# Attention and gated MLP in one kernel: background matmuls dealt one pair to an exp, and layer norm by row tile on GpSimd

## The chip, the cores and the metric

The kernel runs on one core of a Trainium2 chip. The metric is the time of one execution on the device in microseconds (us). Engines are named as in the profile: PE is TensorE's matmuls, PEld its weight loads, DVE is VectorE, ACT ScalarE, POOL GpSimd, and SP the queue that issues the DMAs here.

## The reference

```python
x  = A_x                                  # [1, 2048, 512], bf16
xn = (x - mean) / sqrt(var + 1e-5)        # over the 512 columns
q, k, v = split(xn @ wqkv)                # 32 heads of 16 columns
o  = softmax(q @ k.T / 4) @ v             # per head, 2048 keys
A  = merge_heads(o) @ wo
B  = (relu(xn @ W_gate) * (xn @ W_up)) @ W_down    # 1792 columns inside
out = x + A + B
```

## The kernel before, in words

The sequence of 2048 rows is held as 4 blocks of 512 rows (c4 for queries, b for keys) and 16 row or key tiles of 128 (m, kt). The 32 heads form 4 groups (gg) of two halves (ee) of four heads (j). A head has 16 columns, and two heads share 32 partitions of kT, so kT keeps two copies of k, each with the other head's 16 rows set to zero by a mask (hmask).

The main loop runs over 2048 score tiles (c4, gg, ee, kt, j), each 128 keys by 512 queries. Three tiles make a **unit**; there are 683. For a unit TensorE computes three scores into one half of ps_sc (three banks of PSUM, two halves), ScalarE takes the exp of all three in one instruction into a slot of `ring` (11 slots), and later TensorE multiplies the ring slot with v (PV) into bank 0 of ps_b, where four heads stand at four column places of the array. v has a column of ones, so PV gives the softmax sums too. After 16 key tiles `normalise` copies bank 0 to o_sb, sends the sums through DRAM to all partitions (DMAs rsum, rec_scr and rb), and GpSimd multiplies (oT).

All else is **background** and goes through bank 1 of ps_b: the projections of q and k, the GLU (for each c4, 14 tiles ft of four matmuls with W_up, then four with W_gate), and the output rows (for each 128 rows, 14 matmuls with W_down and 8 with wo). `mm_chain` issues such a chain in operations of two matmuls; I call such an operation a pair. A tile in bank 1 is emptied by VectorE before the next chain starts. In the last block the output rows are summed in parts: a first part without the last head group into `resid`, then the last matmul at the end.

The first units also hold the layer norm of the four blocks (`ln_block`), the transposes of xn, k of the first group and all of v.

What sets the order is a planner. Each operation is recorded with its engine, an estimated duration, its dependencies and a priority; `Graph.run` places them one by one on each engine by these estimates, and the engines then run exactly that order, each waiting on semaphores. Scores have priority u - 2000 and PV u + 4 (PV_LAG), so PV may be late by as much as the ring allows. A background chain gets one priority in units (`later(p, lead, fn)`), and one of its dependencies is the exp of unit p - lead.

## Time and profile before

| | |
|---|---|
| three runs | 1050.02, 1044.48, 1049.61 us; median 1049.61 |
| profiled execution | 1046.26 us, of which the span of the trace is 1044.5 us |
| busy share of the span | ACT 89%, PE 83%, DVE 18%, POOL 5% |
| mean granted TensorE clock | 0.805 |
| exps (ACT, `ring<-ps_sc`, L711) | 683, 929.2 us busy; ScalarE idle before them 69.6 us |
| score matmuls (L699), PV (L729) | 2048 each, 318.0 and 304.3 us busy |
| GLU matmuls (L500, wus and wgs) | 224 each |

The span runs from the first to the last instruction of the trace. Busy time of an engine is the union of its instructions. In a row of the timeline stand the start and duration in us, the engine, the line, the operation, the tile written and those read, and in brackets how long the engine was idle before it and what released it. In a row by stages stand the stretch, its width, and for each engine the busy time with the count of instructions, then the granted TensorE clock (1.00 is full speed), the DMA share and GB/s.

### The profile page before, as it was taken

Reading aid. Unit: us, or ns where it says so; the run is one execution under the profiler, and the core shown is the slowest. Engines: PE = TensorE matmul, PEld = TensorE weight load, DVE = VectorE, ACT = ScalarE, POOL = GpSimd, SP = SyncE. Lnnn points to the kernel's source line nnn. Section 1 sums busy time; section 2 is a strip of 40 time slices with the busy share of each in tenths; the row PEclk is TensorE's granted clock in tenths of the full one; section 3 lists DMA queues with packets and bytes.
Section 4 is the critical chain, followed back from the end, with each engine's and each line's share of the span. In section 5 each row is a group of like instructions: output and inputs, shape, how many; then the busy total and the mean of one; then the engine's idle time right before and its main releaser. Section 6 shows DMA issues by size and latency. Waiting matters only on the chain.

```text
span 1044.5 us, 11864 instructions
## 1 busy us (share of the span) xinstructions
PE 863.8 (83%) x5152; PEld 205.5 (20%) x5152; DVE 191.1 (18%) x323; ACT 932.4 (89%) x687; POOL 51.1 (5%) x46
## 2 busy tenths in 40 slices
PE   4888888888898887888889888888889988888894
PEld 1221221211132111111122111111112212121121
DVE  8732231311002111111001111111100212120001
ACT  3699999999889999999988999999998899999980
POOL 3000000000000000000000000000000000000000
PEclk9998896976599777878569887787758989895587
DMA  8011101110011111100011101111001211110000
GB/s 231 2 31 28 28 18 31 41 31 11 22 36 37 31 36 36 26 21 17 11 31 45 43 12 31 36 31 31 11 21 31 52 42 46 32 26 10 8 26 31
DMA packets 84067, 34.58 MB, mean 33 GB/s; under 512 B 69936, under 2 KB 79920, under 8 KB 84016
## 3 DMA queue, kind: packets, MB, share of 16 engines
q1 hardware_dynamic: 84016, 33.83, 12.4%
q8 instruction: 40, 0.66, 0.3%
q14 instruction: 11, 0.09, 0.0%
HBM read 31.20 MB, written 2.36 MB: 32 GB/s over the span
## 4 chain that ended last, share of the span: by engine, by line
ACT 58%; PE 33%; DMA 4%; DVE 3%; issue 1%; POOL 0%; POOLq 0%; SPq 0%
ACT ring L711 58%; PE ps_b L500 18%; PE ps_sc L699 9%; PE ps_b L729 6%; DMA rb<-rec_scr 2%; DMA rsum<-o_sb 1%; DMA rec_scr<-rrec 1%; DMA wus<-in_B_W_up_dram 1%; DVE stats L442 1%; DVE pid L371 1%; DVE v_aug L533 0%; POOL oT L681 0%; PE ps_sc L500 0%; DVE o_sb L663 0%; DVE kT L525 0%
## 5 line engine op out<-in xcount | busy, mean ns | idle before, releaser
L711 ACT ACTIVATE ring<-ps_sc 128x1536 bf16<-128x1536 f32 (+1 forms) x683 | 929.2, 1555 | 69.6 <-PE ps_sc L699 55.0
L699 PE MATMUL ps_sc<-qT,kT 32*128 32x512 bf16 x2048 | 318.0, 460 | 133.3 <-ACT ring L711 126.4
L729 PE MATMUL ps_b<-ring,v_aug 128*17 128x512 bf16 x2048 | 304.3, 455 | 1.2 <-DVE o_sb L663 1.2
L699 PEld LDWEIGHTS ps_sc<-qT,kT 32*128 32x128 bf16 x2048 | 68.0, 93 | 442.4 <-ACT ring L711 342.6
L729 PEld LDWEIGHTS ps_b<-ring,v_aug 128*17 128x17 bf16 x2048 | 61.8, 89 | 199.4 <-issue 187.6
L595 DVE COPY up_sb<-ps_b 128x512 f32<-128x512 f32 x56 | 38.7, 691 | 315.7 <-PE ps_b L500 315.7
L500 PE MATMUL ps_b<-xnT,wus 128*128 128x512 bf16 x224 | 90.8, 505 | 1.8 <-DMA wus<-in_B_W_up_dram 1.7
L681 POOL TENSOR_TENSOR oT<-o_sb,rb 128x512 bf16<-128x512 f32 x32 | 40.5, 1266 | 956.4 <-DMA rb<-rec_scr 927.1
L500 PE MATMUL ps_b<-xnT,wgs 128*128 128x512 bf16 x224 | 73.8, 421 | 1.9 <-DMA wgs<-in_B_W_gate_dram 0.5
L500 PE MATMUL ps_b<-Wd,hT 128*128 128x512 bf16 x224 | 63.8, 414 | 8.0 <-POOL oT L681 6.3
L599 DVE SCALAR_TENSOR_TENSOR hT<-ps_b,up_sb 128x512 bf16<-128x512 f32 x56 | 38.7, 691 | 105.9 <-PE ps_b L500 105.9
L663 DVE COPY o_sb<-ps_b 128x512 f32<-128x512 f32 x32 | 22.1, 692 | 160.6 <-PE ps_b L729 160.3
L500 PE MATMUL ps_b<-Wo_p,oT 128*128 128x512 bf16 x125 | 33.4, 383 | 0.0
L631 DVE TENSOR_TENSOR ost<-ps_b,xr_sb 128x512 bf16<-128x512 f32 x12 | 8.3, 691 | 116.4 <-PE ps_b L500 116.4
L525 DVE TENSOR_SCALAR kT<-ps_b,hmask 128x512 bf16<-128x512 f32 x32 | 22.5, 746 | 22.1 <-PE ps_b L500 22.1
L500 PEld LDWEIGHTS ps_b<-Wd,hT 128*128 128x128 bf16 x224 | 18.4, 101 | 40.5 <-issue 16.0
L500 PEld LDWEIGHTS ps_b<-xnT,wus 128*128 128x128 bf16 x224 | 14.5, 103 | 39.8 <-issue 33.7
L500 PEld LDWEIGHTS ps_b<-xnT,wgs 128*128 128x128 bf16 x224 | 13.8, 99 | 35.3 <-DVE up_sb L595 19.4
L500 PE MATMUL ps_b<-xnT,Wk 128*128 128x512 bf16 x64 | 18.9, 405 | 1.8 <-DVE xnT L480 0.8
L500 PE MATMUL ps_b<-xnT,Wq 128*128 128x512 bf16 x60 | 19.2, 416 | 0.8
L500 PE MATMUL ps_b<-Wv,xnT 128*128 128x512 bf16 x64 | 16.4, 381 | 1.9 <-DVE v_aug L533 1.0
L512 DVE CAST qT<-ps_b 128x512 bf16<-128x512 f32 x15 | 10.3, 689 | 30.6 <-PE ps_b L500 30.6
(43 smaller groups left out, 108.3 us busy)
## 6 DMA issues: line engine op xcount, KB each, us to landing
rb<-rec_scr SPq DMA_DIRECT2D x32, 256.0 KB
wus<-in_B_W_up_dram SPq DMA_DIRECT2D x56, 128.0 KB, 3.0
wgs<-in_B_W_gate_dram SPq DMA_DIRECT2D x56, 128.0 KB, 2.3
xr_sb<-in_A_x_dram SPq DMA_DIRECT2D x16, 128.0 KB, 2.2
out_dram<-ost SPq DMA_DIRECT2D x16, 128.0 KB, 1.7
Wd<-in_B_W_down_dram SPq DMA_DIRECT2D x1, 1792.0 KB, 11.7
x_sb<-in_A_x_dram SPq DMA_DIRECT2D x3, 512.0 KB, 5.9
x_sb<-in_A_x_dram SPq DMA_DIRECT2D x2, 256.0 KB, 3.0
```

The costliest lines, as they stand in the source:

```text
L371: G.op("DVE", 100, lambda e: e.tensor_scalar(pid[:], pid[:], 16, None, op0=ALU.bitwise_and), reads=[t_pid], writes=[t_pid], prio=-890)
L442: G.op("DVE", 620, lambda e, m=m: e.bn_stats(stats[:, m, :], xs(m)), reads=[t_xm[m]], writes=[t_st], prio=pr)
L500: ins = e.matmul(bank_of(tile, sub), l(), r(), start=(i == 0), stop=(i == n - 1))
L512: G.op("DVE", 690, lambda e: e.tensor_copy(qT[:, tq.slot, :], bank_of(t, sub)), reads=[t], writes=[tq], prio=prio)
L525: G.op("DVE", 690, lambda e, ee=ee, dst=dst: e.tensor_scalar(dst, bank_of(t, sub), hmask[:, ee:ee + 1], None, op0=ALU.mult), reads=[t, t_m ...
L595: G.op("DVE", 690, lambda e: e.tensor_copy(up_sb[:, tup.slot, :], bank_of(tu)), reads=[tu], writes=[tup], prio=pr)
L599: G.op("DVE", 690, lambda e: e.scalar_tensor_tensor(out=hT[:, FT * th.slot + ft, :], in0=bank_of(tg), scalar=0.0, in1=up_sb[:, tup.slot, : ...
L663: G.op("DVE", 690, lambda e: e.tensor_copy(o_sb[:, to.slot, :], ps_b[:, 0, :]), reads=[tp], writes=[to], prio=-950, name="oev%d" % n)
L681: G.op("POOL", 1200, lambda e: e.tensor_tensor(oT[:, tn.slot, :], o_sb[:, to.slot, :], rb[:, trb.slot, :], ALU.mult), reads=[to, trb], wri ...
L699: ins = e.matmul(ps_sc[:, 3 * ts.slot + i, :], kT[32 * j:32 * j + 32, 2 * gg + ee, 128 * kt:128 * kt + 128], qT[32 * j:32 * j + 32, t_q[(c ...
L711: return e.activation(ring[:, UNIT * tr.slot:UNIT * tr.slot + n, :], ps_sc[:, 3 * ts.slot:3 * ts.slot + n, :], ACTF.Exp, scale=0.25)
L729: ins = e.matmul(ps_b[32 * j:32 * j + VN, 0, :], v_aug[:, kt, 8 * gg + 2 * j + ee, 0:VN], ring[:, UNIT * tr.slot + i, :], start=(kt == 0), ...
```

## The change

**One pair to a unit.** `job(want, n, fn, lead)` takes the place of `later`. All background chains are sorted by the unit at which they are wanted, and each pair gets a slot of its own, one unit behind the one before at the least. The slot is the pair's priority, and `after` makes the pair depend on the exp of the unit before the slot. The output rows of a block take 11 slots for each 128 rows, from unit 10 of the next block on. Those of the last block come before its end: a part with five of the eight head groups, a part with two, and at the end the last one. The GLU's places are moved too.

**PV by key tile.** The four PV matmuls of a key tile (j = 0 to 3) are issued together once the fourth is exponentiated, in place of three for each unit. The ring has 13 slots.

**Layer norm by row tile.** The addition of eps, the power and the normalisation are done by GpSimd for each row tile apart; in block 0 ScalarE copies each tile's transposes out of PSUM. Before, VectorE normalised and the power was done once for four tiles.

**k split by GpSimd.** VectorE copies k to `kp` once, and GpSimd writes the two masked copies. Before, VectorE wrote both from PSUM.

**Start.** TensorE runs 14 matmuls of zeros at first. The memsets of v_aug's ones and of Wo_p wait for the exps of units 1 and 29, and so does the load of Wd for the latter. The first load of x is split in two. Eight of the oT tiles use the space of x_sb, and the output tiles that of xn_sb.

```diff
-NRING = 11
+NRING = 13
...
+            if o.after is not None and int(o.after) > 0:
+                o.order.add(self.units[min(int(o.after), len(self.units)) - 1])
...
-        G.op("POOL", 2500, lambda e: e.memset(v_aug[:, :, :, DH:VN], 1.0), writes=[t_vones], prio=-500)
-        G.op("POOL", 4200, lambda e: e.memset(Wo_p[:], 0.0), writes=[t_woz], prio=-400)
+        G.op("POOL", 2500, lambda e: e.memset(v_aug[:, :, :, DH:VN], 1.0), writes=[t_vones], prio=-500, after=2)
+        G.op("POOL", 4200, lambda e: e.memset(Wo_p[:], 0.0), writes=[t_woz], prio=20, after=30)
...
-            G.op("DVE", 150, lambda e: e.tensor_scalar(vare[:, sl], mv[:, sl, 1], EPS, None, op0=ALU.add), ...
-            G.op("POOL", 1000, lambda e: e.tensor_tensor(rstd[:, sl], vare[:, sl], expo[:, :], ALU.pow), ...
+                G.op("POOL", 100, lambda e, m=m: e.tensor_scalar(vare[:, m:m + 1], mv[:, m, 1:2], EPS, None, op0=ALU.add), ...
+                G.op("POOL", 300, lambda e, m=m: e.tensor_tensor(rstd[:, m:m + 1], vare[:, m:m + 1], expo[:, 0:1], ALU.pow), ...
...
-                    G.op("DVE", 420, lambda e, m=m, t=t_n: e.tensor_scalar(
+                G.op("POOL", 450, lambda e, m=m, t=t_n: e.tensor_scalar(
                         xn_sb[:, t.slot, :], xs(m), mv[:, m, 0:1], rstd[:, m:m + 1], op0=ALU.subtract, op1=ALU.mult),
...
+            G.op("DVE", 690, lambda e: e.tensor_copy(kp[:, tkp.slot, :], bank_of(t, sub)), reads=[t], writes=[tkp], prio=prio)
+                G.op("POOL", 450, lambda e, ee=ee: e.tensor_scalar(dsts[ee], kp[:, tkp.slot, :], hmask[:, ee:ee + 1], None, op0=ALU.mult), ...
...
+            for _ in range(14):
+                ins = e.matmul(ps_b[:, 1, :], zeros[:, 0:128], zeros[:], start=True, stop=True)
...
-            a = upos(c4) + (40 if c4 == 0 else 28)
-            z = upos(c4 + 1) - (12 if c4 < NB - 1 else 50)
+            a = upos(c4) + (20 if c4 == 0 else 60)
+            z = upos(c4 + 1) - (8 if c4 < NB - 1 else 56)
             for ft in range(FT):
-                later(a + (z - a) * ft / FT, 8, lambda pr, od, c4=c4, ft=ft: glu(c4, ft, pr, od))
+                job(a + (z - a) * ft / FT, 4, lambda s, c4=c4, ft=ft: glu(c4, ft, s))
             for i in range(4):
                 if c4 < NB - 1:
-                    later(upos(c4 + 1) + 8 + 4 * i, 6, lambda ...: out_rows(c4, i, pr, od, range(8), True, True))
+                    job(upos(c4 + 1) + 10 + 12 * i, 11, lambda ...: out_rows(c4, i, range(8), True, True, slots=s), 2)
                 else:
-                    later(upos(c4, 3, 1, 0) + 8 + 4 * i, 6, lambda ...: out_rows(c4, i, pr, od, range(7), True, False))
+                    job(upos(c4 + 1) - 54 + 10 * i, 10, lambda ...: out_rows(c4, i, range(5), True, False, slots=s), 2)
+                    job(upos(c4 + 1) - 12 + i, 1, lambda ...: out_rows(c4, i, [5, 6], False, False, slots=s), 1)
+        jobs.sort(key=lambda j: j[0])
+        plan, cur = [], 0.0
+        for want, n, fn, lead in jobs:
+            s = []
+            for _ in range(n):
+                cur = max(cur, want)
+                s.append(cur)
+                cur += 1.0
+            plan.append((s[0] - lead, s, fn))
...
-                G.op("PE", 330 * (i1 - i0) / 3, pv, reads=[tr, t_vones] + [...], writes=[tp], prio=u + PV_LAG, name="pv%d" % u)
+            for i, t in enumerate(cl):
+                where[t] = (tr, i)
+                if t[4] == 3:
+                    pv_group(t[:3], t[3], u)
```

In the three excerpts of the order below, a row is a line of the kernel, an operation, the tile written and those read, its size, and how many stand in a row. Before, L699 is the scores, L729 PV and L500 the background; now they are L760, L736 and L510.

TensorE's order at the output rows of c4 = 1, which stand some ten units into c4 = 2, before:

```order
L729 MATMUL ps_b<-ring,v_aug 17x512 x3
L500 MATMUL ps_b<-Wd,hT 128x512 x2
L699 MATMUL ps_sc<-qT,kT 128x512 x3
L500 MATMUL ps_b<-Wd,hT 128x512 x4
L699 MATMUL ps_sc<-qT,kT 128x512 x3
L500 MATMUL ps_b<-Wd,hT 128x512 x4
L699 MATMUL ps_sc<-qT,kT 128x512 x3
L500 MATMUL ps_b<-Wd,hT 128x512 x4
L500 MATMUL ps_b<-Wo_p,oT 128x512 x2
L699 MATMUL ps_sc<-qT,kT 128x512 x3
```

and now:

```order
L736 MATMUL ps_b<-ring,v_aug 17x512 x4
L760 MATMUL ps_sc<-qT,kT 128x512 x6
L510 MATMUL ps_b<-Wd,hT 128x512 x2
L736 MATMUL ps_b<-ring,v_aug 17x512 x4
L760 MATMUL ps_sc<-qT,kT 128x512 x3
L510 MATMUL ps_b<-Wd,hT 128x512 x2
L736 MATMUL ps_b<-ring,v_aug 17x512 x4
L760 MATMUL ps_sc<-qT,kT 128x512 x3
```

Between two groups of scores stood up to six background matmuls and no PV; now there are two, and PV goes on between them.

TensorE's order at the end of the program, before:

```order
L699 MATMUL ps_sc<-qT,kT 128x512 x2
L500 MATMUL ps_b<-Wd,hT 128x512 x10
L500 MATMUL ps_b<-Wo_p,oT 128x512 x7
L729 MATMUL ps_b<-ring,v_aug 17x512 x12
L500 MATMUL ps_b<-Wd,hT 128x512 x14
L500 MATMUL ps_b<-Wo_p,oT 128x512 x7
L729 MATMUL ps_b<-ring,v_aug 17x512 x14
```

and now:

```order
L760 MATMUL ps_sc<-qT,kT 128x512 x3
L736 MATMUL ps_b<-ring,v_aug 17x512 x4
L760 MATMUL ps_sc<-qT,kT 128x512 x2
L736 MATMUL ps_b<-ring,v_aug 17x512 x8
L510 MATMUL ps_sc<-Wo_p,x_sb 128x512
```

The output rows of the last block stood behind the last scores; now only PV and the last matmuls with wo do.

GpSimd's order at the start, before:

```order
L370 IOTA pid 128x2
L367 AFFINE_SELECT ident<-ident 128x128
L382 MEMSET v_aug 128x512
L383 MEMSET Wo_p 128x4096
L448 TENSOR_TENSOR rstd<-vare,expo 128x4 x4
```

and now, from the normalisation of block 1's last two tiles on (the same three rows stand ahead of it for each two tiles before):

```order
L452 TENSOR_SCALAR vare<-mv 128x1 x2
L454 TENSOR_TENSOR rstd<-vare,expo 128x1 x2
L461 TENSOR_SCALAR xn_sb<-x_sb,mv,rstd 128x512 x2
L452 TENSOR_SCALAR vare<-mv 128x1
L454 TENSOR_TENSOR rstd<-vare,expo 128x1
L387 MEMSET v_aug 128x512
L542 TENSOR_SCALAR kT<-kp,hmask 128x512
```

GpSimd had two memsets and four powers there; now it has three operations for every row tile, the v_aug memset in their midst, and the masks of k behind it.

More of the change, by code (lines that the diff above doesn't have):

```diff
@@ new lines, in ln_block @@
+            first = b == 0
+            t_rs = [Tile() for _ in range(4)]
+            for i in range(4):
+                m = 4 * b + i
+                t_st, t_mv, t_ve = Tile(), Tile(), Tile()
+                G.op("DVE", 640, lambda e, m=m: e.bn_stats(stats[:, m, :], xs(m)), reads=[t_xm[m]], writes=[t_st], prio=pr)
+                G.op("DVE", 120, lambda e, m=m: e.bn_aggr(mv[:, m, :], stats[:, m, :]), reads=[t_st], writes=[t_mv], prio=pr - 0.1)
+                G.op("POOL", 100, lambda e, m=m: e.tensor_scalar(vare[:, m:m + 1], mv[:, m, 1:2], EPS, None, op0=ALU.add),
+                     reads=[t_mv], writes=[t_ve], prio=pr)
+                G.op("POOL", 300, lambda e, m=m: e.tensor_tensor(rstd[:, m:m + 1], vare[:, m:m + 1], expo[:, 0:1], ALU.pow),
+                     reads=[t_ve, t_expo], writes=[t_rs[i]], prio=pr)
```

356 lines of the change are left out of this document (183 added, 173 removed).

## The prediction

> **What bounds the kernel now.** I read the busy shares first, then ScalarE by stages, then single units in the timeline.
>
> ```profile
> span 1044.5 us, 11864 instructions
> ...
> PE 863.8 (83%) x5152; PEld 205.5 (20%) x5152; DVE 191.1 (18%) x323; ACT 932.4 (89%) x687; POOL 51.1 (5%) x46
> ```
>
> ScalarE is the busiest, and nearly all of it is the 683 exps. What an exp costs when nothing delays it, and what the clock is with and without background matmuls, stands in two stretches (time, width, PE, PEld, DVE, ACT, POOL busy, clock):
>
> ```profile
> 120.40:141.70 21.30, 19.26 (x131) 5.12 (x128) 8.13 (x13) 21.30 (x17) 1.27 (x1) 1.00 0.21 51
> 497.40:520.00 22.60, 19.24 (x102) 3.36 (x102) 0.00 (x0) 22.60 (x18) 1.26 (x1) 0.50 0.03 12
> ```
>
> In the first ScalarE never idles: 17 exps are counted, one lies across a cut, so 16 units in 21.30 us, 1.331 us each. 131 matmuls are 48 of scores, 48 of PV and 35 of background, a pair per unit, and the clock is 1.00. In the second there is no background and the clock is 0.50; that costs nothing, since scores and PV alone fit. The floor is 683 x 1.331 = 909.1 us. ScalarE over the whole loop, cut where the order puts other work:
>
> ```profile
> 21.20:53.50 32.30, 21.81 (x16) 0.95 0.12 15
> 53.50:275.90 222.40, 216.40 (x160) 0.84 0.11 27
> 275.90:327.50 51.60, 44.03 (x33) 0.90 0.15 43
> 327.50:512.90 185.40, 174.96 (x129) 0.77 0.11 26
> 512.90:587.00 74.10, 65.27 (x49) 0.83 0.12 33
> 587.00:772.30 185.30, 174.74 (x129) 0.75 0.10 25
> 772.30:824.90 52.60, 44.17 (x33) 0.82 0.13 37
> 824.90:935.00 110.10, 108.32 (x81) 0.91 0.16 39
> 935.00:1017.80 82.80, 79.49 (x60) 0.63 0.05 17
> ```
>
> The units in the rows are 16, 160, 32, 128, 48, 128, 32, 80 and 59 (an exp across a cut is counted twice). Width less units x 1.331 is what each row loses: 11.0 (first units), 9.4 (c4 = 0), 9.0, 10.2 and 10.0 (the three blocks of output rows), 15.0 and 14.9 (GLU of c4 = 1 and 2), 3.6 (GLU of c4 = 3) and 4.3 (its output rows): 87.4 us. So 21.2 before the first exp + 909.1 + 87.4 + 26.7 behind the last = 1044.4. Why GLU loses:
>
> ```profile
> 848.75 0.61 PE L699 MATMUL ps_sc<-qT,kT 32*128 32x512 bf16 x3
> 849.29 0.60 PE L729 MATMUL ps_b<-ring,v_aug 128*17 128x512 bf16 x3
> 849.82 1.03 PE L500 MATMUL ps_b<-xnT,wus 128*128 128x512 bf16 x2
> 850.79 0.61 PE L699 MATMUL ps_sc<-qT,kT 32*128 32x512 bf16 x3
> ...
> 852.68 0.39 PE L699 MATMUL ps_sc<-qT,kT 32*128 32x512 bf16 x3
> 853.00 0.39 PE L729 MATMUL ps_b<-ring,v_aug 128*17 128x512 bf16 x3
> 853.33 0.60 PE L500 MATMUL ps_b<-xnT,wgs 128*128 128x512 bf16 x2
> 853.86 0.39 PE L699 MATMUL ps_sc<-qT,kT 32*128 32x512 bf16 x3
> ```
>
> A unit with a pair takes 2.04 us on TensorE at the low clock (848.75 to 850.79) and 1.18 at the full one (852.68 to 853.86). Only the second is under 1.331. After some units without a pair the clock has fallen, and the next burst of four pays until it rises. The price by the length of the gap: 327.5 to 512.9 has 11 gaps of 4 to 6 free units and one of 3 in the order, 587.0 to 772.3 has 10 and one, so (15.0 + 14.9) / 22 = 1.35 each. 824.9 to 935.0 has five gaps of 3 and four of 2 for its 3.6 us: 0.72 for a gap of 3 if they bear all, 0.40 if all nine share. I take 0.55. Check on c4 = 0: six long gaps and three of 3 give 9.8, the row says 9.4.
>
> **Output rows dealt out.** Before, up to 6 background matmuls stand between two groups of scores, and the first waits for the last oT:
>
> ```profile
> 774.09 0.70 DVE o_sb L663
> ...
> 783.73 1.27 POOL oT L681
> ```
>
> From the copy of the last PV result to the end of oT it is 10.9 us, 8.2 units. The order had the waiting matmul 7 units behind that PV in c4 = 0, 1 and 2; now it is 9, 9 and 10. So the wait goes, and the clusters' 29.2 us with it: a pair per unit at full clock fits, as 120.4 shows. What is late next is the clock: each block follows idle units, which I price as one long gap. PV by key tile costs nothing: it turns three groups of three into three groups of four over four units, and the four go to the array's four column places as three do.
>
> **GLU dealt out.** The same pairs, nearer together. Gaps in the new order: c4 = 0 two of 3 and seven longer, 10.6 us (before 9.4); c4 = 1 eight of 3 and four longer (its output rows' entry counted), 9.8; c4 = 2 nine and three, 9.0; c4 = 3 one and one, 1.9, since from its GLU to the last ten units there is a pair in nearly every unit. Together 31.3. For DMAs and evacuations that collide with the dense order I add 2. k, q, the fourth resid pass and the later oT stay hidden: k's mask pass has 14 units and more between its slot and its use.
>
> **The end.** Now output rows stand between the last exp and the last PV:
>
> ```profile
> 1016.63 2.33 PE L500 MATMUL ps_b<-Wd,hT 128*128 128x512 bf16 x10
> ...
> 1025.90 1.03 PE L729 MATMUL ps_b<-ring,v_aug 128*17 128x512 bf16 x14
> ```
>
> They go to earlier units. The last PV starts 0.15 after the last exp in place of 1025.90, 8.1 after it, and has 8 matmuls for 14 (-0.4): 26.7 becomes 18.3.
>
> **The head.** Rows of GpSimd, VectorE, TensorE, ScalarE and of a load of x:
>
> ```profile
> 1.36 2.28 POOL L382 MEMSET v_aug<- 128x512 bf16 x1
> 3.24 3.81 POOL L383 MEMSET Wo_p<- 128x4096 bf16 x1
> 10.34 1.02 POOL L448 TENSOR_TENSOR rstd<-vare,expo 128x4 f32<-128x4 f32 x1 [3.29 <-DVE vare L447]
> ```
>
> ```profile
> 1.36 5.71 DVE L371 TENSOR_SCALAR pid<-pid 128x2 int32<-128x2 int32 x1
> ...
> 7.25 0.68 DVE L442 BATCH_NORM_STATS2 stats<-x_sb 128x6 f32<-128x512 bf16 x1
> ```
>
> ```profile
> 16.54 1.86 PE L500 MATMUL ps_sc<-xnT,Wq 128*128 128x512 bf16 x4 [1.21 <-ACT xnT L479]
> 18.20 1.73 PE L500 MATMUL ps_b<-xnT,Wk 128*128 128x512 bf16 x4
> ```
>
> ```profile
> 21.21 5.48 ACT L711 ACTIVATE ring<-ps_sc 128x1536 bf16<-128x1536 f32 x4 [2.18 <-PE ps_sc L699]
> ```
>
> ```profile
> x_sb<-in_A_x_dram SPq DMA_DIRECT2D x2, 256.0 KB, 3.0
> ```
>
> The pid operation ends within 0.02 us of the second memset's end (7.07, 7.05): I read it as held by GpSimd. With that memset moved, VectorE starts when x lands, about 3 us (an estimate from the 256 KB row, issue at 0.7). Four row tiles of statistics at 0.7 to 0.8 reach 6.2. The Trainium skill, SBUF — State Buffer, Who interferes with whom, says that a VectorE tensor_scalar in a two-port mode and a GpSimd instruction exclude each other for the whole instruction; the trace's 5.71 agrees. Were it the operation's own cost instead, statistics would start at 7.3 as now and the sum would be about 4 us more.
>
> Then GpSimd does each row tile: add 0.15, power, normalise. The power of one element is between 1.02 / 4 = 0.26 and 1.02; I take 0.40. Normalising 512 elements lies between the memset's eighth, 0.48, and oT's 1.27 with two f32 inputs; I take 0.80, between both. So 1.35 per tile (0.89 to 2.45). From 4.6 in batches of two: 7.3 and 10.0. Transposes and copy take 1.2 (TensorE waited 1.21 for a copy of twice the size, row 16.54), and from q's start to the first exp it is 4.7 as now (16.54 to 21.21): first exp at 16.0 (12.5 to 20.5) for 21.2. In that stretch TensorE's queue now has two transposes of block 1 ahead of the first scores; their tiles leave GpSimd at 12.7, so they hold nothing unless a tile takes nearly 2 us, and that is in the upper end. I give the heating nothing, because from its end near 7 to q near 11 stand transposes alone, and behind such transposes q took 1.86 for four matmuls (row 16.54), where two take 0.60 at the full clock. The Trainium skill, TensorE: Matmul & The Clock Gate, Part 1, has the clock rise after some 3.4 us of activity and fall after one idle window; by that rule too the heat is lost before q. If it held, q and k would take 1.5 us less by the pace of the row at 853.33.
>
> In the first units GpSimd's order is: the tiles of blocks 0 and 1 (done at 15.4), two steps of block 2's first tile, whose x lands when block 0's space is free (near 16), the v_aug memset (2.28, end 19.9), then k's mask for block 1 at 20.7. Unit 5 needs it by 16.0 + 5 x 1.331 = 22.7: nothing lost. Before the mask for block 2 stand eight normalisations, seven powers and additions and a mask: with it 20.7 + 6.4 + 3.9 + 1.6 = 32.6, latency 0.6, due for unit 10 at 29.3: 3.9 lost. With 1.5 for TensorE's v matmuls 5.4 (1 to 17) for 11.0.
>
> **Sum.** 16.0 + 909.1 + 5.4 + 31.3 + 2 + 18.3 = 982.1 of span; the profiled execution took 1046.26 against a span of 1044.5, 1.8 more, so 984 in round numbers. That execution is 3.35 below the median shown (1049.61) and within the three (1044.48 to 1050.02).
>
> **Rivals.** *Gaps of three all let the clock fall.* For it: PV's passes are a quarter fewer, so TensorE does less in a gap. Against: gaps of 3 cost under half a long one now. Twenty gaps at 1.35 for 0.55: +16, 1000.
> *GpSimd is the bound of the first units.* At 2.45 a tile the first exp is at 20.5 and the stalls 17: +16, 1000. For it: its rows of two f32 inputs; against: one input and bf16 here.
> *The single evacuation bank.* Each chain starts when VectorE has emptied bank 1:
>
> ```profile
> PEld ps_b L500 <- DVE up_sb L595: 20.9, 54, 0.5
> ```
>
> 0.39 a time, 0.15 of it slack; over 112 GLU chains +27, 1011. Against: 120.4 has such chains and no loss.
> *Slower: the long dense runs go low.* Some 242 units stand in unbroken runs of pairs. At the low clock each loses 2.04 - 1.33 = 0.71, all of them 172, 1156; it is slower than before from 88 such units on. For it: fewer PV passes. Against: clock 1.00 at a pair per unit.
> *The dealing brings nothing* and only head, first units and end gain: 1046.3 - 5.2 - 5.6 - 8.4 = 1027. Against: the order shows the clusters gone.
>
> **Chances.** Forecast 0.60 (own range 970 to 995), three-gaps 0.14, GpSimd 0.11, bank 0.07, nothing 0.04, slower 0.04. From 964 to 1008 the first three are in. A change of 0.5% is about what a measurement of this kernel can tell: faster 0.94, same 0.02, slower 0.04.
>
> **What would show it.** Right: the first exp near 16; exps without gaps through the output rows at clock 1.00; GLU of c4 = 1 and 2 still falling to 0.50 between bursts, less often; c4 = 3 at 1.00 to the end; the last PV directly behind the last exp. Wrong: ScalarE waiting for GpSimd's masks far past unit 10; clock 0.50 in runs of pairs; TensorE waiting for oT, weights or bank 1.

## The result, and the profile after

The changed kernel takes 1008.78 us in the median of three runs (1008.53 to 1008.92), where the kernel before took 1049.61 (1044.48 to 1050.02): ratio 0.9625, interval 0.9579 to 0.9671. It is faster, as forecast, but 24.8 us slower than the 984.0 predicted, and 0.8 above the upper end of the range, 1008. The first lines of its page:

```profile
span 1007.0 us, 11864 instructions
...
PE 779.0 (77%) x5078; PEld 184.7 (18%) x5166; DVE 173.1 (17%) x292; ACT 929.3 (92%) x690; POOL 138.5 (14%) x120
```

GpSimd's busy time has gone from 51.1 to 138.5 us, VectorE's from 191.1 to 173.1. ScalarE by stages (time, width, busy time of ScalarE with its instructions, granted TensorE clock, DMA share, GB/s):

```profile
0.00:22.80 22.80, 4.37 (x8) 0.70 0.45 138
22.80:72.00 49.20, 22.71 (x17) 0.72 0.20 59
...
293.40:358.70 65.30, 64.58 (x49) 0.91 0.11 31
358.70:516.00 157.30, 152.81 (x114) 0.83 0.13 32
...
802.40:989.10 186.70, 186.69 (x140) 0.98 0.14 35
989.10:1007.00 17.90, 0.00 (x0) 0.50 0.14 45
```

From the third row on it is the forecast: output rows (293.4 to 358.7) in which ScalarE idles 0.7 us, GLU of c4 = 1 (358.7 to 516.0) at a clock that still falls, c4 = 3 (802.4 to 989.1) at 0.98 and without a pause. The first two rows are not: the first exp starts at 22.8 for 16.0, and the first 16 units take 49.2 us where 16 x 1.331 = 21.3 would do. What ScalarE waits for there, and how long (in brackets):

```profile
22.80 2.79 ACT L772 ACTIVATE ring<-ps_sc 128x1536 bf16<-128x1536 f32 x2 [2.45 <-PE ps_sc L760]
29.27 1.45 ACT L772 ACTIVATE ring<-ps_sc 128x1536 bf16<-128x1536 f32 x1 [3.68 <-PE ps_sc L760]
...
60.90 2.79 ACT L772 ACTIVATE ring<-ps_sc 128x1536 bf16<-128x1536 f32 x2 [11.94 <-PE ps_sc L760]
```

and GpSimd in the same time:

```profile
6.22 4.17 POOL L461 TENSOR_SCALAR xn_sb<-x_sb,mv,rstd 128x512 bf16<-128x512 bf16 x2
10.37 0.41 POOL L452 TENSOR_SCALAR vare<-mv 128x1 f32<-128x1 f32 x2
10.73 1.08 POOL L454 TENSOR_TENSOR rstd<-vare,expo 128x1 f32<-128x1 f32 x2
11.82 4.17 POOL L461 TENSOR_SCALAR xn_sb<-x_sb,mv,rstd 128x512 bf16<-128x512 bf16 x2
...
56.55 2.09 POOL L461 TENSOR_SCALAR xn_sb<-x_sb,mv,rstd 128x512 bf16<-128x512 bf16 x1
58.62 3.11 POOL L542 TENSOR_SCALAR kT<-kp,hmask 128x512 bf16<-128x512 bf16 x2
```

It hardly rests from 4.8 to 61.7. Block 0's last tile leaves it at 16.0 (forecast 10.0); q starts 1.8 behind it (1.2), and the first exp 5.0 behind q (4.7). The masks of k for block 2, which unit 10 needs, stand at 58.62, behind the last normalisation. The wait of 11.94 us is that of unit 10, and it ends when the first of these masks is done, at 60.2 (forecast 32.6). Its operations by line (minimum, median and maximum in ns, then the first and last start in us):

```profile
L461 POOL TENSOR_SCALAR xn_sb<-x_sb,mv,rstd x16: 2076/2091/2099, 6.2 to 56.5; 128x512 bf16<-128x512 bf16 x16
...
L454 POOL TENSOR_TENSOR rstd<-vare,expo x16: 549/569/572, 5.1 to 55.9; 128x1 f32<-128x1 f32 x16
...
L542 POOL TENSOR_SCALAR kT<-kp,hmask x30: 1559/1565/1577, 33.4 to 237.6; 128x512 bf16<-128x512 bf16 x30
```

A normalisation is 2.09 us, a row tile with its addition (0.2) and power (0.57) some 2.85. At the other end the last PV follows the last exp at once, as forecast:

```profile
989.14 0.61 PE L736 MATMUL ps_b<-ring,v_aug 128*17 128x512 bf16 x4 [0.31 <-ACT ring L772]
```

All runs by the terms of the prediction's sum, in us. A loss is the time between two exp starts less the units between them times 1.331; behind the last exp stands the rest of the span. The row of the kernel before has the figures of the prediction's stages. Medians are of the timed runs.

| kernel | median | first exp | lost in units 0 to 15 | lost in the rest | behind the last exp |
|---|---|---|---|---|---|
| before | 1049.61 | 21.2 | 11.0 | 76.4 | 26.7 |
| predicted | 984.0 | 16.0 | 5.4 | 33.3 | 18.3 |
| after | 1008.78 | 22.8 | 27.9 | 29.1 | 17.9 |
| e1 normalisation on VectorE | 979.85 | 15.9 | 6.2 | 28.9 | 18.2 |
| e2 planner knows GpSimd's durations | 1002.04 | 22.3 | 21.0 | 25.1 | 17.9 |
| e4 before, normalisation on GpSimd | 1071.90 | 32.3 | 20.6 | 81.0 | 26.5 |
| e5 = e1 without heat | 980.82 | 16.0 | 6.2 | 25.5 | 18.2 |
| e6 = e1 with free units filled | 959.23 | 16.0 | 6.2 | 7.5 | 18.1 |
| e7 = e1 with GLU spread | 974.86 | 15.3 | 7.2 | 24.0 | 17.9 |
| e8 = e1 with PV by unit | 979.42 | 16.1 | 7.2 | 27.7 | 17.9 |
| e9 = e1 with rows clustered | 994.14 | 16.6 | 5.9 | 43.6 | 17.9 |
| e14 = e1 with rows earlier | 986.77 | 15.8 | 6.2 | 36.1 | 18.4 |
| e15 = e9 and e14 together | 996.04 | 16.9 | 6.6 | 47.2 | 17.7 |
| e11 = e6 with the start mended | 960.10 | 14.8 | 8.0 | 7.5 | 17.9 |
| e13 = e11 with the Wo_p memset later | 957.11 | 15.5 | 4.4 | 7.5 | 18.2 |

Against the prediction the first exp and the first units are 29.3 us over (6.8 and 22.5), and the rest and the end 4.6 under (4.2 and 0.4): together the 24.8 us that the kernel is late, up to rounding.

e3, e10 and e12 are told below. One of the four executions of e3, the profiled one, was disturbed (1829 us), so the median of its three others stands for it, and its terms are not read.

### The profile page after: what moved, and what is told of

Same layout as the page of the kernel before. It is cut to its first block, busy times and chain, and to the rows that moved or that the text cites. A ratio compares the mean times of both kernels' runs of the same rounds, so it can differ in the third digit from the quotient of the medians.

```text
span 1007.0 us, 11864 instructions
## 1 busy us (share of the span) xinstructions
PE 779.0 (77%) x5078; PEld 184.7 (18%) x5166; DVE 173.1 (17%) x292; ACT 929.3 (92%) x690; POOL 138.5 (14%) x120
## 4 chain that ended last, share of the span: by engine, by line
ACT 78%; PE 14%; POOL 5%; issue 1%; another core or an unknown queue 1%; DVE 1%; DMA 0%; ACTq 0%; SPq 0%
ACT ring L772 78%; PE ps_b L510 6%; PE ps_sc L760 5%; POOL xn_sb L461 3%; PE ps_b L736 3%; POOL rstd L454 1%; POOL kT L542 1%; POOL vare L452 0%; DMA x_sb<-in_A_x_dram 0%; DVE xn_sb L648 0%; DMA rsum<-o_sb 0%; DVE kp L539 0%; PE ps_sc L510 0%; PE ps_b L478 0%
## 5 line engine op out<-in xcount | busy, mean ns | idle before, releaser
L760 PE MATMUL ps_sc<-qT,kT 32*128 32x512 bf16 x2048 | 300.9, 435 | 171.0 <-ACT ring L772 138.8
L736 PE MATMUL ps_b<-ring,v_aug 128*17 128x512 bf16 x2048 | 224.7, 432 | 5.0 <-DVE o_sb L707 2.0
L760 PEld LDWEIGHTS ps_sc<-qT,kT 32*128 32x128 bf16 x2048 | 67.6, 93 | 440.3 <-ACT ring L772 376.3
L722 POOL TENSOR_TENSOR x_sb<-o_sb,rb 128x512 bf16<-128x512 f32 x20 | 25.4, 1269 | 556.6 <-DMA rb<-rec_scr 556.6
L736 PEld LDWEIGHTS ps_b<-ring,v_aug 128*17 128x17 bf16 x2048 | 49.4, 88 | 198.8 <-issue 188.0
L510 PE MATMUL ps_b<-xnT,wus 128*128 128x512 bf16 x194 | 76.1, 469 | 5.4 <-issue 5.2
L510 PE MATMUL ps_b<-xnT,wgs 128*128 128x512 bf16 x213 | 70.8, 413 | 2.1 <-issue 1.8
L510 PE MATMUL ps_b<-Wd,hT 128*128 128x512 bf16 x206 | 66.5, 399 | 3.1 <-issue 3.1
L542 POOL TENSOR_SCALAR kT<-kp,hmask 128x512 bf16<-128x512 bf16 x30 | 46.6, 1566 | 65.6 <-DVE kp L539 64.1
L722 POOL TENSOR_TENSOR oT<-o_sb,rb 128x512 bf16<-128x512 f32 x12 | 15.2, 1270 | 233.5 <-DMA rb<-rec_scr 233.5
L648 DVE TENSOR_TENSOR xn_sb<-ps_b,xr_sb 128x512 bf16<-128x512 f32 x12 | 8.3, 692 | 146.8 <-PE ps_b L510 146.8
L461 POOL TENSOR_SCALAR xn_sb<-x_sb,mv,rstd 128x512 bf16<-128x512 bf16 x16 | 33.4, 2091 | 0.2
L510 PE MATMUL ps_b<-Wo_p,x_sb 128*128 128x512 bf16 x71 | 22.6, 387 | 11.8 <-POOL x_sb L722 10.9
L510 PE MATMUL ps_b<-xnT,Wk 128*128 128x512 bf16 x60 | 21.1, 444 | 1.1 <-issue 0.8
L510 PE MATMUL ps_b<-Wv,xnT 128*128 128x512 bf16 x60 | 20.7, 449 | 1.2 <-issue 0.4
L510 PEld LDWEIGHTS ps_b<-xnT,wus 128*128 128x128 bf16 x224 | 13.7, 103 | 34.0 <-issue 31.7
L510 PEld LDWEIGHTS ps_b<-xnT,wgs 128*128 128x128 bf16 x224 | 13.1, 99 | 31.3 <-issue 23.0
L510 PE MATMUL ps_b<-xnT,Wq 128*128 128x512 bf16 x52 | 17.5, 407 | 1.3 <-issue 1.3
```

The source lines that it names most:

```text
L461: G.op("POOL", 450, lambda e, m=m, t=t_n: e.tensor_scalar(xn_sb[:, t.slot, :], xs(m), mv[:, m, 0:1], rstd[:, m:m + 1], op0=ALU.subtract, o ...
L510: ins = e.matmul(bank_of(tile, sub), l(), r(), start=(i == 0), stop=(i == n - 1))
L542: G.op("POOL", 450, lambda e, ee=ee: e.tensor_scalar(dsts[ee], kp[:, tkp.slot, :], hmask[:, ee:ee + 1], None, op0=ALU.mult), reads=[tkp, t ...
L648: G.op("DVE", 690, lambda e: e.tensor_tensor(xn_sb[:, to_.slot, :], bank_of(t, sub), xr_sb[:, txr.slot, :] if first else resid(i), ALU.add ...
L722: G.op("POOL", 1200, lambda e: e.tensor_tensor(oT_of(tn), o_sb[:, to.slot, :], rb[:, trb.slot, :], ALU.mult), reads=[to, trb], writes=[tn] ...
L736: ins = e.matmul(ps_b[32 * j:32 * j + VN, 0, :], v_aug[:, kt, 8 * gg + 2 * j + ee, 0:VN], ring[:, UNIT * tr.slot + i, :], start=(kt == 0), ...
```

## Experiments on the lost 25 us

**e1.** One operation goes back to VectorE; all else of the change stays.

```diff
-                G.op("POOL", 450, lambda e, m=m, t=t_n: e.tensor_scalar(
+                G.op("DVE", 420, lambda e, m=m, t=t_n: e.tensor_scalar(
                     xn_sb[:, t.slot, :], xs(m), mv[:, m, 0:1], rstd[:, m:m + 1], ...
```

> The changed kernel with one operation of each row tile, the normalisation, back on VectorE; GpSimd keeps the addition, the power, the masks of k and the memsets. Theory A (the 16 normalisations of 2.09 us on GpSimd are what the forecast mis-sized, they hold the first exp back and then the first units): first exp near 15 to 16, loss of the first 16 units 4 to 9 us, the rest unchanged, 978 to 990 us. Rival B (GpSimd's masks of k, 1.57 us each, and its one-element powers are enough to hold the first units): first exp near 17, loss of the first units still 20 and more, about 1000 us. Rival C (something else, such as x's arrival or the v projections): within 5 us of 1008.8.

979.85 us (978.56 to 981.93; 0.936 of before, interval 0.9335 to 0.9385). Theory A holds. Its ScalarE by stages, and the operation on VectorE:

```profile
0.00:15.94 15.94, 4.37 (x8) 0.89 0.65 198
15.94:43.45 27.51, 22.02 (x16) 1.00 0.15 39
43.45:960.40 916.95, 902.00 (x667) 0.86 0.13 32
```

```profile
L461 DVE TENSOR_SCALAR xn_sb<-x_sb,mv,rstd x16: 380/412/647, 6.2 to 36.2; 128x512 bf16<-128x512 bf16 x16
```

0.41 us for 2.09: the same operation is five times as long on GpSimd. With it back, the first exp stands at 15.9 for the predicted 16.0, and the first units lose 6.2 for the predicted 5.4. Against the changed kernel that is 6.9 and 21.6, together 28.5 of the 28.9 us between the two medians.

**e2 and e3** ask whether it was the order of GpSimd's queue, or the masks, in place of the normalisation. e2 tells the planner the measured durations; e3 writes the masks on VectorE.

```diff
-                G.op("POOL", 450, lambda e, m=m, t=t_n: e.tensor_scalar(      # and vare 100, rstd 300, kT 450
+                G.op("POOL", 2090, lambda e, m=m, t=t_n: e.tensor_scalar(     # and vare 200, rstd 560, kT 1570
```

```diff
-                G.op("POOL", 450, lambda e, ee=ee: e.tensor_scalar(dsts[ee], kp[:, tkp.slot, :], hmask[:, ee:ee + 1], ...
+                G.op("DVE", 420, lambda e, ee=ee: e.tensor_scalar(dsts[ee], kp[:, tkp.slot, :], hmask[:, ee:ee + 1], ...
```

> The changed kernel with the planner's durations for GpSimd set to the measured ones (addition 200 ns, power 560, normalisation 2090, mask 1570), so that it orders the queues knowing them. The work on GpSimd is the same. Theory A (the amount of work on GpSimd, 45 us of row tiles and 9 us of masks, is the cause): the last mask cannot come before about 55 us, the unit that needs it is due near 43, so at least 12 of the 28 us stay: 993 to 1006 us, first exp unchanged at 22 to 23. Rival D (the wrong estimates make a bad order, masks behind row tiles that are not yet due): most of the 28 us returns, 980 to 988 us.

> The changed kernel with the masks of k on VectorE and everything else as it is; GpSimd keeps the whole row tile of 2.84 us. Theory A (row tiles): first exp unchanged at 22 to 23; tiles of block 3 still leave GpSimd near 50, the units that need them are due near 43; loss of the first 16 units 12 to 20 us, 992 to 1002 us in all. Rival B (masks): loss of the first units 5 us or less, 982 to 988 us. If the masks only wait in a queue that would be late anyway, within 5 us of 1008.8.

e2 takes 1002.04 us (997.63 to 1005.38; 0.9568 of before, 0.9532 to 0.9603) and e3 998.21 (996.74 to 1000.50; 0.9536, 0.9505 to 0.9567). Both are in theory A's ranges. A better order wins 6.7 us and the masks 10.6; in both the sixteen row tiles, some 45 us of GpSimd (16 x 2.85), stay where they were.

**e4** puts the normalisation alone on GpSimd, in the kernel before.

```diff
-                    G.op("DVE", 420, lambda e, m=m, t=t_n: e.tensor_scalar(
+                    G.op("POOL", 420, lambda e, m=m, t=t_n: e.tensor_scalar(
```

> The kernel before with one edit: the normalisation of each row tile on GpSimd, planned at the same 420 ns; statistics, power in batches of four, split of k and background order stay. Theory A (normalisation on GpSimd takes 2.09 us against 0.41 on VectorE): the first exp 5 to 7 us later, the first 16 units 0 to 12 us more, slower by 5 to 18 us: 1054 to 1068 us. Rival E (the cost comes only with the rest of the change, the row-by-row powers and the masks): within 3 us of 1049.6.

1071.90 us, 1.028 of before (1.0203 to 1.0357): the one operation makes the kernel before slower too, and by more than the 1054 to 1068 us expected (first exp 11.1 later for 5 to 7, first units 9.6 more). The trace shows why the first exp is so late: block 0's four normalisations end at 19.7, but in TensorE's order the transposes of three tiles of block 1 stand ahead of q, and the third had to wait for GpSimd until 27.1.

**e10** asks why it takes 2.09 us. Nine forms on scratch data, each twice:

```diff
+            e.tensor_scalar(sco, scr[:], 0.5, None, op0=ALU.mult),                               # L755
+            e.tensor_scalar(sco, scr[:], 0.5, 1.0, op0=ALU.subtract, op1=ALU.mult),              # L756
+            e.tensor_scalar(sco, scr[:], hmask[:, 0:1], None, op0=ALU.mult),                     # L757
+            e.tensor_scalar(sco, scr[:], hmask[:, 0:1], hmask[:, 1:2], ...subtract, ...mult),    # L758; 256 and 128
+            ...                                                              # elements L759, L760; f32 out L761
+            e.tensor_copy(sco, scr[:]),                                                          # L762
+            e.tensor_tensor(sco, scr[:], scr[:], ALU.mult),                                      # L763
```

> The changed kernel with the normalisation on VectorE, and with nine forms of a GpSimd operation on scratch data, twice each, from exp unit 345 on, where GpSimd has almost nothing else to do; only their durations are asked for. Known so far, on 128x512 bf16: one multiplication by a per-partition scalar 1.57 us, subtraction and multiplication by two 2.09. Theory N (each per-partition scalar operand costs about 0.5 us): with immediates in their place both forms fall to about 1.05, two immediates no dearer than one. Rival O (each arithmetic step costs about 0.5 us, whatever its operand): one immediate 1.57, two 2.09. Both: the time goes with the elements, so 128 elements take about 0.6 us, a quarter of 2.09 and a small fixed part.

```profile
L755 POOL TENSOR_SCALAR scf<-scr x2: 1492/1494/1497, 481.7 to 519.1; 128x512 bf16<-128x512 bf16 x2
L756 POOL TENSOR_SCALAR scf<-scr x2: 1932/1932/1933, 483.3 to 520.7; 128x512 bf16<-128x512 bf16 x2
L757 POOL TENSOR_SCALAR scf<-scr,hmask x2: 1565/1568/1570, 509.1 to 522.8; 128x512 bf16<-128x512 bf16 x2
L758 POOL TENSOR_SCALAR scf<-scr,hmask x2: 2077/2080/2082, 510.8 to 524.4; 128x512 bf16<-128x512 bf16 x2
L759 POOL TENSOR_SCALAR scf<-scr,hmask x2: 1213/1216/1219, 513.0 to 526.6; 128x256 bf16<-128x256 bf16 x2
L760 POOL TENSOR_SCALAR scf<-scr,hmask x2: 788/790/792, 514.3 to 538.1; 128x128 bf16<-128x128 bf16 x2
L761 POOL TENSOR_SCALAR scf<-scr,hmask x2: 2072/2072/2072, 515.2 to 539.0; 128x512 f32<-128x512 bf16 x2
L762 POOL COPY scf<-scr x2: 609/609/609, 517.3 to 541.2; 128x512 bf16<-128x512 bf16 x2
L763 POOL TENSOR_TENSOR scf<-scr x2: 1038/1038/1038, 518.0 to 541.9; 128x512 bf16<-128x512 bf16 x2
```

Rival O is nearer, though not all of the price is steps. Two steps with immediates take 1.93 us and one 1.49, so the second arithmetic step costs 0.44; a scalar from memory in place of an immediate adds 0.07 each. The time goes with the elements (0.43 us for each 128, about 0.36 fixed) and the output type changes nothing. A copy is 0.61, the product of two tensors 1.04: both cheaper than one multiplication by a number. So the kind of operation counts beside the steps; why a tensor_scalar of one step is dearer than a tensor_tensor of one step stays open. The Trainium skill, GPSIMD Engine Reference, 4.1 Engine selection, sends elementwise work to VectorE and calls GpSimd about twice as slow with two inputs and roughly at line rate with one. The runs agree that the normalisation belongs on VectorE, but not that one input is at line rate: it has one tensor as input and takes 2.09 us on GpSimd against VectorE's 0.41. No run has one operation with two inputs, on the same operands, on both engines.

## Experiments on the rest of the sum

All of these stand on e1.

**e5** leaves the early heating of TensorE out.

```diff
-        G.op("PE", 6000, heat, reads=[t_zero], writes=[tw0], prio=-900)
```

> The changed kernel with the normalisation on VectorE (979.9 us, first exp at 16.0 in its profile), and without the 14 early matmuls that heat TensorE. Theory A (the heat is lost before q, the granted clock is 0.50 again from 9 us on): first exp within 0.3 us of 16.0, 978 to 982 us. Rival F (the heat shortens q and k of the first block): first exp 1 to 2 us later, 981 to 984 us.

980.82 us (977.16 to 987.33), first exp at 15.99 for 15.94. Theory A holds: the heat does not last. In e1 the granted clock is 1.00 up to 11 us, 0.62 from 11 to 12 and 0.50 from 12 to 14, so it falls while q begins, later than the 9 us that the expectation names. The four matmuls of q and of k behind the heat (first two rows, e1) and without it (e5):

```profile
10.99 1.68 PE L510 MATMUL ps_sc<-xnT,Wq 128*128 128x512 bf16 x4 [0.69 <-ACT xnT L484]
12.46 1.91 PE L510 MATMUL ps_b<-xnT,Wk 128*128 128x512 bf16 x4
```

```profile
11.19 1.89 PE L510 MATMUL ps_sc<-xnT,Wq 128*128 128x512 bf16 x4 [0.69 <-ACT xnT L484]
12.88 1.83 PE L510 MATMUL ps_b<-xnT,Wk 128*128 128x512 bf16 x4
```

**e6** gives every free unit a pair on zeros; **e7** adds no work and puts half of each free stretch between the two halves of a GLU group.

```diff
+        taken = {int(x) for _, s, _ in plan for x in s}
+        for u in range(16, NU - 4):
+            if u not in taken:
+                ...    # one pair: e.matmul(ps_b[:, 1, :], zeros[:, 0:128], zeros[:], start=True, stop=True), twice
```

```diff
+            room = (jobs[i + 1][0] if i + 1 < len(jobs) else cur) - cur - n
+                if n == 4 and k == 2:
+                    cur += max(0, int(room / 2 + 0.5))
```

> The changed kernel with the normalisation on VectorE, and in every exp unit that has no background pair a pair of matmuls on zeros into the free evacuation bank, whose result nobody reads; all the work of the reference stays. Theory G (the 18.9 us that units 16 to 672 lose there, beyond 1.331 each, are the price of bursts that meet TensorE at the low clock): clock 1.00 nearly throughout, loss of these units under 5 us, 963 to 970 us. Rival H (they are lost to chains that wait for the one evacuation bank, to DMAs and evacuations): the pairs only add chains, 980 to 990 us. Rival I (TensorE without a pause is throttled or delays the scores): above 990 us.

> The changed kernel with the normalisation on VectorE, and each group of four GLU pairs cut in the middle, half of the free units put between its two halves: in c4 = 1 and 2 the gaps of three and four become gaps of one and two; no work is added. Theory G (only a gap long enough to leave a stretch of about 3.4 us with under two pairs lets the clock fall): loss of units 176 to 512 falls from about 13 us to under 5, about 968 to 973 us. Rival J (every gap has its price, whatever its length): twice the gaps, 980 to 988 us. Rival H (bank): as now, 978 to 982 us.

e6 takes 959.23 us (958.95 to 959.85; 0.916 of before, 0.9141 to 0.9178), 20.6 less than e1 by adding work. Theory G holds in its cause, with the clock at 1.00 from unit 16 to the last exp; its figures were off. By e1's trace units 16 to 671 lose 28.6 us, not 18.9, so the gain is larger and the time lies below the expected 963; and the loss left is 7.3 there, not under 5. ScalarE by stages:

```profile
43.00:939.00 896.00, 895.53 (x667) 1.00 0.13 33
```

The loss of the rest falls from 28.9 to 7.5 us, so at least 21.4 of it were the low clock. The 7.5 show no wait: ScalarE is busy for 895.53 of 896.00 us, and the exps follow one another evenly, 1.343 us apart in the median. So neither the one evacuation bank nor DMAs cost anything one can see. e7 takes 974.86 (971.81 to 975.73) and falls between the theories: units 176 to 511 lose 11.4 for the 16.9 of e1's trace, not under 5. Shorter gaps help (rivals J and H are out), but in that stretch the burst behind a gap of two free units still lost over 0.2 us in 11 of 19 cases.

**e8** issues PV by unit again.

```diff
-                if t[4] == 3:
-                    pv_group(t[:3], t[3], u)
+            for key in dict.fromkeys(t[:3] for t in cl):
+                pv_unit(key, [t for t in cl if t[:3] == key], u)
```

> The changed kernel with the normalisation on VectorE, and with the PV matmuls of each exp unit issued behind it as before the change (three at a time, two thirds of the units' groups covering two key tiles), not four at a time by key tile. The forecast gave this part nothing: 977 to 983 us. Rival K (a third more passes keep TensorE active in the gaps): the clock falls less often, 970 to 976 us. Rival L (passes of three cost time in units with a pair): 985 us and more.

979.42 us (978.72 to 980.52) for 979.85: the part costs and brings nothing that one can measure, as forecast.

**e9, e14 and e15** undo in part the dealing of the output rows, their later start, and both. The edit of e9 takes every chain of ten pairs or more, so also the parts of the last block.

```diff
-                cur += 1.0
+                cur += 1.0 / 3 if n >= 10 else 1.0
+            cur = float(int(cur + 0.99))
```

```diff
-                    job(upos(c4 + 1) + 10 + 12 * i, 11, ...
+                    job(upos(c4 + 1) + 7 + 12 * i, 11, ...
```

> The changed kernel with the normalisation on VectorE (979.9 us), and with the output rows dealt out three pairs to an exp unit in place of one; GLU, q, k, the place where the rows begin and all else stay. Theory P (the dealing itself is what took the three blocks of output rows from 29 us of loss to nothing: a unit with three pairs takes about 2.24 us on TensorE at the full clock, 1.18 with one): some 58 such units lose up to 0.9 us each, 1005 to 1030 us. Rival M (the blocks lost their time to the wait for the last oT, which the later start alone removes): 978 to 988 us.

> The changed kernel with the normalisation on VectorE (979.9 us), and with the three inner blocks of output rows beginning three exp units earlier, still one pair per unit. Theory U (the first row waits for the last oT, 8.2 units behind the last PV, and the order then has it some 6 units behind): TensorE waits 2 to 4 us for oT in each block, of which the scores already made hide 1 to 2; 981 to 988 us. Rival V (the wait is hidden by the scores ahead, or the oT comes earlier than 8.2 units): 978 to 981 us.

> Both: output rows dealt in clusters (994.1 us for that alone) and beginning three units earlier. If the two parts only add, 994 plus what the early rows alone cost; if the forecast's 29 us need both, as it said, 1003 to 1012 us, with the loss of each inner block near 9 to 10 us as before the change.

e9 takes 994.14 us (990.62 to 996.69), between the two theories. Its trace tells why theory P was too high: the planner did not put three pairs between two groups of scores but two, and at the full clock two fit.

```profile
292.42 1.35 PE L510 MATMUL ps_b<-Wd,hT 128*128 128x512 bf16 x4
...
293.70 0.39 PE L761 MATMUL ps_sc<-qT,kT 32*128 32x512 bf16 x3
294.03 1.04 PE L510 MATMUL ps_b<-Wd,hT 128*128 128x512 bf16 x4
...
295.00 0.39 PE L761 MATMUL ps_sc<-qT,kT 32*128 32x512 bf16 x3
```

Scores follow at 1.30 us (293.70 to 295.00), under 1.331, with PV put off. What the clusters cost is mostly at their start, where the clock is still low after the free units: in its first cluster it is 0.50 up to 274.5 us and 1.00 from 276.6 on, the first three units lose 2.3 us and the others nothing. By the exp starts the stretches of the three inner blocks lose 11.8 us more than in e1, and the units from 630 on, with the last block's parts, 3.8 more. e14 takes 986.77 (984.95 to 991.70), theory U. TensorE's waits for oT in the matmuls of the output rows, e14 first and then the kernel before (total, times, longest; in e14 the end of the program, 11.3, is in it):

```profile
PE ps_b L510 <- POOL x_sb L722: 17.2, 4, 11.3
```

```profile
PE ps_b L500 <- POOL oT L681: 6.3, 3, 3.3
```

17.2 - 11.3 = 5.9 for three blocks, as the 6.3 of before, and 6.9 us of time. e15 takes 996.04 (995.13 to 999.24): the parts do not even add, and the 29 us are not reached. They were for rows that stood back to back with up to six matmuls between two groups of scores, which these edits do not bring back. So the wait was worth about 7 of the 29 us and clusters of this milder kind about 12.

The kernel before has a third loss there, which the prediction does not name. ScalarE's waits show it (total, times, longest):

```profile
ACT ring L711 <- PE ps_b L729: 12.4, 6, 2.3
```

Six times, twice in each of the three blocks, an exp waits for PV, which had been put off behind the background matmuls, to free a slot of the ring. In the changed kernel one such wait of 0.3 us is left, and e8, e9, e14 and e15 have none. So neither PV by key tile (e8) nor one pair to a unit (e9) is needed by itself to be rid of it; no run takes the ring back from 13 slots to 11, so whether the two slots did it stays open.

**e12** is on the head: in the kernel before, the two memsets wait for the masks of VectorE.

```diff
-lambda e: e.memset(v_aug[:, :, :, DH:VN], 1.0), writes=[t_vones]
+lambda e: e.memset(v_aug[:, :, :, DH:VN], 1.0), reads=t_masks, writes=[t_vones]
-lambda e: e.memset(Wo_p[:], 0.0), writes=[t_woz]
+lambda e: e.memset(Wo_p[:], 0.0), reads=t_masks, writes=[t_woz]
```

> The kernel before with the two GpSimd memsets (v_aug, Wo_p) made to wait for VectorE's masks, nothing else moved. Reading Q of the forecast (the 5.71 us of the pid operation are GpSimd's memsets holding VectorE): the pid operation takes 0.1 to 0.3 us, statistics start when x lands near 3 us; the power then waits for the memsets, which end near 8 to 9, so of the 4 us some 1 to 3 show in the first exp (18 to 20 for 21.1). Rival R (the operation is that slow by itself, or waits for data): it still takes over 5 us, first exp unchanged or later.

```profile
1.37 0.16 DVE L371 TENSOR_SCALAR pid<-pid 128x2 int32<-128x2 int32 x1
...
3.71 3.81 POOL L383 MEMSET Wo_p<- 128x4096 bf16 x1
...
5.57 0.66 DVE L442 BATCH_NORM_STATS2 stats<-x_sb 128x6 f32<-128x512 bf16 x1
...
6.48 1.07 DVE L447 TENSOR_SCALAR vare<-mv 128x4 f32<-128x4 f32 x1
```

The pid operation takes 0.16 us for 5.71, so reading Q was right. The trace shows more: while the memset runs (3.71 to 7.52), statistics keep their 0.66, but the small addition of eps is held until 7.55. The Trainium skill, SBUF — State Buffer, Who interferes with whom, says that a VectorE tensor_scalar in a two-port mode and a GpSimd instruction block each other for the whole instruction, and that a VectorE instruction with at most one SBUF input outside these modes does not contend. The trace agrees for these two forms. The time is 1046.86 us for 1048.62 (ratio 0.9975, 0.9951 to 0.9998), which counts as the same. The gain expected at the first exp (18 to 20) did not come: it is at 20.95 for 21.21, since VectorE's queue has the statistics of block 1, whose x lands late, ahead of block 0's normalisation.

**e11 and e13** are the version that these runs point to: e6, the masks of the first k group from PSUM on VectorE, the v_aug memset on VectorE, and zeros between block 0's transposes.

```diff
-            if (gg, b) == (0, 0):
+            if gg == 0:
-        G.op("POOL", 2500, lambda e: e.memset(v_aug[:, :, :, DH:VN], 1.0), ..., prio=-500, after=2)
+        G.op("DVE", 700, lambda e: e.memset(v_aug[:, :, :, DH:VN], 1.0), ..., prio=-850)
+                    # block 0, behind the transposes of tile i: (5, 3, 2, 2)[i] matmuls of zeros into bank 1
```

> The kernel of the filled free units (959.2 us) with the start mended: the first block group's k masks straight from PSUM on VectorE, the memset of v_aug on VectorE before the first statistics, and matmuls on zeros between the transposes of the first block, so that TensorE does not cool down before q. By the theory that GpSimd's queue costs the first units most of their 6.2 us (4 back) and the low clock q and k some 1.8 us: first exp 14 to 15, loss of the first 16 units 1 to 4 us, 951 to 956 us. Rival: TensorE's v projections bound the first units and the zeros only push the transposes back: 957 to 961 us.

960.10 us (959.10 to 962.29), no gain on 959.23: the expected 951 to 956 was missed, and the time lies in the rival's range. The first exp came at 14.8, with q's four matmuls in 1.03 us for 1.68, so heat that lasts does quicken q; but the first units lost 8.0 for 6.2. e13 asks whether the cause was not the rival's but a memset. The normalisations on VectorE and a memset on GpSimd in e11, and the normalisations of e13, which has that memset 40 units later in the plan, and the loads of Wo_p behind it:

```profile
L463 DVE TENSOR_SCALAR xn_sb<-x_sb,mv,rstd x16: 378/408/3570, 6.5 to 33.6; 128x512 bf16<-128x512 bf16 x16
```

```profile
33.53 3.51 POOL L388 MEMSET Wo_p<- 128x4096 bf16 x1
```

```profile
L463 DVE TENSOR_SCALAR xn_sb<-x_sb,mv,rstd x16: 382/408/415, 6.5 to 34.3; 128x512 bf16<-128x512 bf16 x16
```

```diff
-        G.op("POOL", 4200, lambda e: e.memset(Wo_p[:], 0.0), writes=[t_woz], prio=20, after=30)
+        G.op("POOL", 4200, lambda e: e.memset(Wo_p[:], 0.0), writes=[t_woz], prio=60, after=70)
...
-                    reads=[t_woz], writes=[Tile()], prio=40)
+                    reads=[t_woz], writes=[Tile()], prio=80, after=76)
```

> The kernel with filled free units and mended start (960.1 us), with only the memset of Wo_p and the loads behind it moved from exp unit 30's place in GpSimd's queue to unit 70's. Theory S (in that run the memset ran at 33.5 to 37.0 us and held a VectorE normalisation of block 3 for 3.57 us in place of 0.41, and the units that wait for block 3 lost it): all normalisations 0.4 to 0.7 us, loss of the first 16 units 4 to 6 us for 8.05, 956 to 958 us. Rival T (VectorE's own work, statistics, copies of v and masks, is the bound there): 959 to 961 us.

With little else on GpSimd, the memset had moved up to 33.53, when unit 12 was running, and held one normalisation of block 3 for 3.57 us. It could, because `after` binds the planner alone: an operation is placed behind an exp in the plan, but no wait for that exp is issued, and on the chip it starts as soon as its queue and its data allow. The description of the change, by which memsets and pairs wait for exps, holds for the plan only. With the memset moved away, no normalisation takes more than 0.42, the first units lose 4.4, and the time is 957.11 us (956.57 to 957.25): 0.9134 of before (0.9103 to 0.9164), 51.7 us faster than the changed kernel. Theory S.

## Why the prediction was right or wrong

**Wrong: GpSimd's row tile.** The step that failed is "normalising 512 elements lies between the memset's eighth, 0.48, and oT's 1.27 with two f32 inputs; I take 0.80". It measured 2.09, outside both ends. The bound was chosen by operands (two f32 inputs must be dearer than one of bf16), and e10 shows that the price goes by the kind of operation and its arithmetic steps: a tensor_scalar of one step is at 1.49, already above oT's tensor_tensor, and the normalisation's second step adds 0.44. The same slip put a mask at 0.80 for 1.57; the power was 0.57 for 0.40, inside its bounds. So a tile was 2.85 for 1.35, the first exp came at 22.8 for 16.0, and the first units lost 27.9 for 5.4. The order of GpSimd's queue was as the prediction read it, with block 2's mask behind eight normalisations: it was above all the sizes that put that mask at 60.2 for 32.6. ScalarE waiting for GpSimd's masks is also the prediction's own sign of being wrong, though the long wait comes at unit 10 and not far past it. e1, which takes only this operation away, ends at 979.85, 4 under the forecast.

**The rival named for it was too cheap.** "GpSimd is the bound of the first units" described what happened, but its price of 16 us came from the same bound, 2.45 a tile: first exp 20.5 for the measured 22.8, stalls 17 for 27.9. What it had against it, one input in bf16, was no reason for a low price. It had 0.11 although no row showed that kind of operation on GpSimd.

**Right: the floor, the rest, the end.** 683 x 1.331 held. The rest lost 29.1 for 33.3, the end took 17.9 for 18.3. The GLU's price per gap was a clock price, as read: e6 takes 21.4 us away by keeping TensorE busy. The price of 0.55 for a gap of three is an average of two cases: of the fifteen bursts behind such a gap in e1 (units 176 to 511), six lose 1.0 to 1.7 us and nine at most 0.15, together 7.5. The 2 us for DMAs and evacuations came from no row, and e6 shows no such wait. A pair per unit at the full clock fits (c4 = 3: 186.69 of 186.70 us busy). PV by key tile is worth nothing (e8), heat nothing (e5).

**Right with another split: the 29.2 us of the clusters.** They went, but not only by the two causes named: the wait for oT was worth about 7 (e14), clusters of a milder kind about 12 (e9), and 12.4 were waits for PV to free the ring, which the prediction does not have. The three do not simply add (e15), so that the total came out is in part luck.

**Right: the memset's hold on VectorE** (e12; 0.16 us in the changed kernel too). Its worth in the head could not show, since GpSimd became the bound there.

**The other rivals** did not come: gaps of three that all let the clock fall (six of fifteen cost that in e1, and the rest lost 29.1, where this rival needs 16 more than 33.3), single bank (e6 shows no such loss), dense runs at the low clock (c4 = 3 at 0.98), nothing from dealing (the rest lost 76.4 before).

## What to carry to other kernels

Before an elementwise step moves to GpSimd, price it by a GpSimd row of the same kind of operation with the same number of arithmetic steps, or put no tight upper end on it: what VectorE does in 0.41 us took 2.09 there. An engine that looks idle over the span (5%) can still be the bound of the first 60 us, where all its work falls at once; add up its queue in that stretch at the upper price, and let the rival use a price beyond the forecast's own bound. Where short bursts of matmuls come and go, filling the slots that are still free after the real ones have been dealt out with matmuls that nobody needs can pay (another 20.6 us here).

## What the runs showed of the hardware that I had not expected

A multiplication of 512 bf16 elements per partition by a number takes 1.49 us on GpSimd, a product of two tensors 1.04, a copy 0.61. A GpSimd memset of 3.5 us held a VectorE normalisation for 3.57 us and left statistics beside another memset at 0.66. With TensorE at work all the time one exp starts 1.343 us after the other (median of e6), where the changed kernel has 1.331; no run tells why.
